# Attention and gated convolution in one launch: a new hand-out order of the same 1784 operations

## The chip, the cores and the metric

The kernel runs on one core of one Trainium2 chip. The metric is the device time of one execution in microseconds (us). The core's engines each work through a queue of their own, in order: TensorE (PE; its weight loads are shown apart as PEld), VectorE (DVE), ScalarE (ACT), GpSimd (POOL), and SyncE (SP), which issues all loads and stores. They wait for each other through semaphores, and an instruction that waits holds up everything behind it in its queue.

## What is computed

The reference is an attention with a window and a few global columns, followed by a gated convolution (B = 4, H = 8, S = 768, D = 64, local window 96, 8 global columns; model width 512, 5 taps), all in float32:

```python
scores = scale * q @ k.T + bias            # bias = -slope[h] * distance
scores = where(is_global | is_local, scores, -1e9)
a = exp(scores - max(scores)); a = a / (sum(a) + 1e-9)
x = merge_heads(a @ v)                     # [B, S, 512]
gate = sigmoid(sum_k conv_w[k] * x shifted by k)   # 5 causal taps
val = x @ w_val
out = (gate * val) @ w_out
```

Weights and tap factors arrive in 64-bit float form and are split into 32-bit numbers in the head of the kernel; the large matmuls then use a high and a low part of each factor (three matmuls for one product).

## The kernel before, in words

The rows are cut into 8 phases (4 batches, each in two halves of 3 blocks of 128 rows). A phase has 4 pairs of heads; a pair in a phase is a group (32), and a group's block is a step (96). The text names an operation by a code and its indices:

- Weights, i = 0 to 7 (0 to 3 are w_val, 4 to 7 w_out): WL loads 64-bit words; WA (L552, ACT), W1 (L557), W2 (L562), W3 (L565) and W4 (L571) on DVE make float32 of them; WH (L326 or L328) casts the high part; WS and WP make the low part, on PE (L609 to L611) and ACT or DVE for i below 4, otherwise on POOL. WL2 and SQ (L586) read them again for a check of range.
- Tables: DIST (distances; DVE, L517 and near it), BIAS(h,part) for each head (L532 on ACT, L534 on DVE or POOL).
- Attention, step s, head j of the pair: Lrk, Lrq and LV load keys, queries and values; S(u) are the scores of up to three steps (PE, L685); AM(s,j) adds the bias and takes the row minimum of the negated scores (DVE, L693); EX(s,j) is the exponential with a row sum (ACT, L704, an activation and a read of its accumulator). For two groups q and block k: RG(q,k) adds 1e-9 to the four sums (L711), RC(q,k) is the reciprocal (DVE, L714), NM(s,j) scales the row (L720), PT(q,k) transposes (PE, L734 whole, L737 in tiles), EV(q,k,i) takes it out of PSUM (L326 on ACT, L328 on the others), PV(q,k) multiplies by the values into a PSUM bank x (PE, L765).
- Convolution, group g: HI and HO carry the 4 last columns from one phase to the next (L863; L326 or L328), XH and XL are the high and the low part of x (L326 or L328, L872), CV(g,k) are the five taps (L883 the first on ACT, L881 the others on DVE), SG is the sigmoid in the form of a tanh (ACT, L928).
- Output, phase ph: VM(ph,m,c) is x @ w_val (PE, L935), GM(ph,m) the gate times it (DVE, L944), GH and GL its two parts (L326 or L328; L952), OM the second matmul (PE, L963), OE its evacuation (L975, L977), ST the store (SP, L989).

What sets the order is a list written out in full, the string `ORDER` (lines 53 to 128). `Plan.order()` walks it and emits one operation a word, so each engine's queue holds its operations in the order in which the list names them:

```python
for word in ORDER:
    i = int(word.rstrip("agvst"))
    e = self.ENGINES.get(word[-1]) or next(iter(ops[i][1]))
```

A word is the number of the operation and, where it may run on several engines, the letter of one (a ACT, v DVE, g POOL). While it walks, a cost model in `Plan.order()` guesses when each operation begins. It decides two further things: whether a transpose PT is done whole or in tiles (`self.tiled`), and where PE gets filler matmuls that multiply constants in a wait expected before 95 us: `self.fills` ahead of an operation that opens a PSUM bank, `self.before` ahead of others. No other list of priorities is consulted.

Of the kernel before, what the change touches and what calls it, by code (L numbers as in the profile page):

```python
# [61 lines left out]
    235 468 446g 1132 477 18 469g 1142 444g 449a 28 460 184g 1133 314 31 463 1126v 1137 478 470 1143 487 1152 479v  # L62
    474g 501 264 464 502 471g 196 265 451a 472g 505 452a 480 473g 506 191a 197 266 483g 488 30 205 315 1145a 489g
    509 19 484g 198 1147a 1405 36 482g 490 510 1153a 1156a 1146 192g 1399 1154a 1148 1406 496a 1157 236 200a 481g 35
    1149 495a 493g 503 494g 1158 316 20 1144a 491g 507 1155 1400 492g 195 1150 193g 1407 497a 1159 498a 1408 513 511
    1151 201g 317 504 1160 515 1401 1161v 514 1397 25 199g 1169v 523 267 524 533 534 268 516 206 512 237 517g 1402
    202g 508 1409 525 1412 518 549 526 26 550 522g 1413 499a 553 519g 554 551 1419 527v 557 521g 500a 1414 528 207
    204 532g 558 269 520v 1403g 535 531v 209a 530g 238 208v 529g 1164a 1404v 27 318 536 210g 1165 38 1172a 1420 561
    37 543a 1166 1415 552 211g 562 1421 544a 1173 1410a 1422 1416 1162a 537g 319 571 555 1411g 1423 1417a 1426 1167
    43 559 1418g 572 1432 560 42 1174 573 1427 581 1170a 538 1168 1433 556 542g 1163 545a 541g 1434 582 546a 1424g  # L70
    1175 45 1177a 539g 1428 563 1171 540g 564 239 1176 583 565g 1185v 1425g 584 566 320 597 574 598 270 567g 601
    548a 50 570v 585g 547a 568g 602 32 271 599 605 575g 44 569g 576 603 606 272 586 579g 578v 590g 580v 240 1178a
    587g 600 588g 1180v 321 1186a 577g 33 609 1429 592a 591v 1188a 49 610 1435 1179 1430a 52 619 322 620 621 1189
# [36 lines left out]
    1320 977a 1008 1633 1329 978a 1033 1011g 1034 1629 1035 1001g 1037 1324v 347 1630a 1325 1634 1015 1631 1326 1640  # L110
# [1238 lines left out]
```

## Time and profile before

| | |
|---|---|
| median of 3 runs | 251.1 us (251.1, 250.1, 251.37) |
| the profiled execution | 249.76 us, its span 248.0 us |
| instructions | 10366 |
| granted clock of TensorE, mean | 0.998 |
| PE busy | 238.8 us (96% of the span) |
| PEld busy | 204.7 us (83%) |
| DVE busy | 213.4 us (86%) |
| ACT busy | 179.6 us (72%) |
| POOL busy | 130.4 us (53%) |
| DMA | 45.94 MB, 185 GB/s on average |
| the chain that ended last | PE 80%, DVE 12%, POOL 4% of the span |

How to read it: the profile comes from one execution. Its span runs from the first to the last recorded instruction; 1.76 us of the execution's own time lie outside. An engine counts as busy while an instruction of its own is under way. L12 is line 12 of the kernel's file. The chain is followed back from the last instruction, at each step to what released it or to the instruction before it on its engine.

### The profile page before, as it was taken

Reading aid. Unit: us, or ns where it says so; the run is one execution under the profiler, and the core shown is the slowest. Engines: PE = TensorE matmul, PEld = TensorE weight load, DVE = VectorE, ACT = ScalarE, POOL = GpSimd, SP = SyncE. Lnnn points to the kernel's source line nnn. Section 1 sums busy time; section 2 is a strip of 40 time slices with the busy share of each in tenths; the row PEclk is TensorE's granted clock in tenths of the full one; section 3 lists DMA queues with packets and bytes.
Section 4 is the critical chain, followed back from the end, with each engine's and each line's share of the span. In section 5 each row is a group of like instructions: output and inputs, shape, how many; then the busy total and the mean of one; then the engine's idle time right before and its main releaser. Section 6 shows DMA issues by size and latency. Waiting matters only on the chain.

```text
span 248.0 us, 10366 instructions
## 1 busy us (share of the span) xinstructions
PE 238.8 (96%) x4037; PEld 204.7 (83%) x4041; DVE 213.4 (86%) x822; ACT 179.6 (72%) x600; POOL 130.4 (53%) x264
## 2 busy tenths in 40 slices
PE   8998788999999999999999999999999999999993
PEld 3556577888899888988899788898899889988993
DVE  3997999998979989898989989898979979989620
ACT  3999899998998488877967589886678388422202
POOL 6989999999317530364064533455419741810220
PEclk9999999999999999999999999999999999999999
DMA  5999598161298054529558289791079507200303
GB/s 181 401 397 386 200 336 284 36 187 52 61 306 306 3 186 186 167 100 272 187 172 256 84 272 345 221 312 48 7 261 402 200 25 227 73 4 0 127 8 134
DMA packets 23095, 45.94 MB, mean 185 GB/s; under 512 B 2688, under 2 KB 13696, under 8 KB 23040
## 3 DMA queue, kind: packets, MB, share of 16 engines
q1 hardware_dynamic: 23040, 45.21, 53.4%
q8 instruction: 34, 0.56, 0.9%
q14 instruction: 21, 0.17, 0.2%
HBM read 38.91 MB, written 6.29 MB: 182 GB/s over the span
## 4 chain that ended last, share of the span: by engine, by line
PE 80%; DVE 12%; POOL 4%; DMA 1%; issue 1%; ACT 0%; SPq 0%; DVEq 0%; POOLq 0%
PE o L963 26%; PE val L935 25%; PE x L765 11%; PE s L685 9%; PE pt L734 5%; PE pt L737 4%; DVE gate L881 3%; DVE t L693 3%; POOL p L720 3%; DVE wh L562 2%; DMA counts_i<-in_counts 1%; DVE xl L872 1%; DVE wy L557 1%; POOL wvh L328 1%; DVE wy L565 1%
## 5 line engine op out<-in xcount | busy, mean ns | idle before, releaser
L720 POOL TENSOR_SCALAR p<-p,rs 128x168 f32<-128x168 f32 (+1 forms) x152 | 66.3, 450 | 55.1 <-DVE rs L714 36.4
L704 ACT ACTIVATE p<-t,mins 128x168 f32<-128x168 f32 (+1 forms) x192 | 81.5, 430 | 13.8 <-DVE mins L693 12.2
L881 DVE SCALAR_TENSOR_TENSOR gate<-x,cwt,gate 128x384 f32<-128x384 f32 x128 | 76.2, 614 | 1.1
L693 DVE CUSTOM_DVE_ANT_0 t<-s,bias 128x168 f32<-128x168 f32 (+1 forms) x192 | 54.1, 318 | 7.6 <-PE s L685 7.5
L935 PE MATMUL val<-xh,wvh 128*128 128x384 f32 x128 | 44.4, 347 | 0.2 <-DVE gate L944 0.2
L326 ACT COPY a<-pt 128x384 f32<-128x384 f32 (+2 forms) x79 | 35.3, 473 | 11.7 <-PE pt L734 7.6
L935 PE MATMUL val<-xl,wvh 128*128 128x384 f32 x128 | 41.8, 327 | 0.0
L935 PE MATMUL val<-xh,wvl 128*128 128x384 f32 x128 | 41.7, 326 | 0.0
L963 PE MATMUL o<-woh,gh 128*128 128x512 f32 (+1 forms) x100 | 39.1, 391 | 0.0
L704 ACT ACTIVATION_READ_ACCUMULATOR p<-t,mins 128x1 f32 x192 | 37.6, 196 | 0.0
L963 PE MATMUL o<-woh,gl 128*128 128x512 f32 (+1 forms) x100 | 37.2, 372 | 0.0
L963 PE MATMUL o<-wol,gh 128*128 128x512 f32 (+1 forms) x100 | 37.1, 371 | 0.0
L765 PEld LDWEIGHTS x<-a,v 56*64 56x64 f32 (+1 forms) x2112 | 33.7, 135 | 4.0 <-issue 1.1
L685 PE MATMUL s<-rk,rq 64*64 64x168 f32 (+1 forms) x768 | 35.8, 304 | 1.1 <-issue 0.9
L765 PE MATMUL x<-a,v 56*64 56x64 f32 (+1 forms) x2112 | 35.8, 219 | 0.8 <-DVE x L863 0.7
L685 PEld LDWEIGHTS s<-rk,rq 64*64 64x64 f32 x768 | 25.8, 132 | 8.9 <-issue 6.0
L952 POOL TENSOR_TENSOR gl<-gate,gh 128x384 fp32r<-128x384 f32 x24 | 24.1, 1008 | 11.8 <-ACT gh L326 5.0
L935 PEld LDWEIGHTS val<-xh,wvh 128*128 128x128 f32 x128 | 24.2, 189 | 1.8 <-DVE gate L944 0.5
L935 PEld LDWEIGHTS val<-xl,wvh 128*128 128x128 f32 x128 | 24.2, 189 | 0.5 <-DVE xl L872 0.2
L935 PEld LDWEIGHTS val<-xh,wvl 128*128 128x128 f32 x128 | 24.2, 189 | 0.0
L944 DVE SCALAR_TENSOR_TENSOR gate<-gate,val 128x384 f32<-128x384 f32 x32 | 17.4, 549 | 4.7 <-PE val L935 4.5
L963 PEld LDWEIGHTS o<-wol,gh 128*128 128x128 f32 x100 | 18.9, 189 | 2.4
(101 smaller groups left out, 351.0 us busy)
## 6 DMA issues: line engine op xcount, KB each, us to landing
v<-in_vw SPq DMA_DIRECT2D x40, 384.0 KB, 5.6
rq<-in_qT SPq DMA_DIRECT2D x32, 192.0 KB, 5.3
rk<-in_kT SPq DMA_DIRECT2D x16, 252.0 KB, 4.8
out<-ob SPq DMA_DIRECT2D x15, 256.0 KB, 4.8
w<-in_wb SPq DMA_DIRECT2D x7, 512.0 KB, 5.8
again<-in_wb SPq DMA_DIRECT2D x7, 512.0 KB, 5.9
rk<-in_kT SPq DMA_DIRECT2D x16, 200.0 KB, 4.9
out<-ob SPq DMA_DIRECT2D x12, 128.0 KB, 1.8
```

The costliest lines, as they stand in the source:

```text
L326: nc.scalar.copy(dst, src)
L685: nc.tensor.matmul(T["s", step[g, k], j][half], T["rq", g][r, k * P + i * HQ : k * P + (i + 1) * HQ], T["rk", g][r, c0 : c0 + n], start=Tr ...
L693: nc.vector.tensor_tensor_reduce(out=t[:, :n], in0=T["s", s, j], in1=bias[:, h, :P] if n == P else bias[:, h, P:], op0=ALU.add, op1=ALU.mi ...
L704: nc.scalar.activation(p_of(s, j), T["t", s, j][:, :n].rearrange("p (c w) -> p c w", c=pieces(s)[0]), AF.Exp, bias=mins[:, s, j : j + 1], ...
L720: engine(e).tensor_scalar(out=pr, in0=pr, scalar1=rs, scalar2=1.0, op0=ALU.mult, op1=ALU.mult)
L734: nc.tensor.transpose(pt[n // 4][:, n % 4 * P : n % 4 * P + P], src, ident)
L765: nc.tensor.matmul(T["x", 2 * q + r][j * D : (j + 1) * D, c0 : c0 + HQ], v[rows, slot], a[rows, i, n * j + c], start=c == 0, stop=c == use ...
L881: nc.vector.scalar_tensor_tensor(out=gt, in0=src, scalar=w, in1=gt, op0=ALU.mult, op1=ALU.add)
L935: nc.tensor.matmul(T["val", ph, m], (wvh, wvh, wvl)[r][:, c, m * P : (m + 1) * P], woven((T["xh", g], T["xl", g], T["xh", g])[r][:, : size ...
L944: nc.vector.scalar_tensor_tensor(out=t, in0=t, scalar=1.0, in1=T["val", ph, m].rearrange("p (b a) -> p a b", a=2), op0=ALU.add, op1=ALU.mult)
L952: engine(e).tensor_sub(tile_of(("gl", ph, m), [P, HT], F32R, "gl", G_B)[:, :n], T["g", ph, m], T["gh", ph, m][:, :n])
L963: nc.tensor.matmul(T["o", ph, k, h], (T["gh", ph, c], T["gl", ph, c], T["gh", ph, c])[r][:, cols], woven((woh, woh, wol)[r][:, c])[:, h * ...
```

## The change

The string `ORDER` is replaced as a whole (76 lines by 76). The numbers name the same 1784 operations; nothing else in the file differs. 171 of DVE's, ACT's and POOL's operations change engine among these three (54 of them NM, 27 each way): DVE has 603 of them in place of 607, ACT 411 in place of 410, POOL 249 in place of 246; within each queue the order differs too. PE's 365 operations move by 0.33 places on average and by 7 at most, SP's 156 loads and stores by up to 18. Walking the new list, the cost model puts in 16 fillers (8 and 8) where the old list had 18 (12 and 6): two ahead of WS(2) and one each ahead of PT(1,0) and PT(1,2) are gone, two ahead of S(5) are new. One transpose in tiles is PT(13,1) where it was PT(13,2).

The first nine lines of each list and those that hold the last gate parts:

```diff
@@ -50,82 +50,82 @@
-    114 0 118 1125 1134 140 2 3 120 1g 122 123 138a 130g 119 128g 149 141 124g 142 133g 131a 143 126a 8 229 125g
-    127a 132a 7 144 135a 4 137a 357 145g 358 359 361 115 362 360 365 363 129g 116 366 158 150 146g 151 117 10 228
-    367 152 9 230 134g 364 5 153 155a 147 154g 369 370 371 379 380 372 389 381 373v 167 374 160 156 382 15 375g 390
-    148a 377v 383g 14 376g 391 161 378g 159 231 162 368 164g 384 163v 392 309 388g 157a 405 406 165 139g 407 409 176
-    387g 400a 410 136g 413 411 169 393g 16 399a 414 385g 415 170 17 232 386g 168 6 171 173g 412 394 261 172v 408 310
-    396g 166a 417 418 395g 174 185 419 427 397g 428 420 398g 437 402a 438 421g 22 429 178 422 401a 179 233 426g 430
-    11 180 175a 21 425g 311 431v 453 416 423g 432 454 262 404a 433g 457 403a 458 436g 187 439 435g 263 461 12 440
-    462 182g 188 24 455 434g 234 1129a 23 189 424g 1135a 194 441v 1138a 1130 183g 177 312 1139 1127a 465 1140 186
-    181g 13 1131 447a 29 448a 466 456 475 190g 313 1128 1136a 476 459 1398 442 485 467 443g 486 203 450a 1141 445g
...
-    1688 110 1112 1108v 1107g 1368a 1694 1113v 1095v 1366a 1685v 1689 1114 1369 1690 1116g 1367 1695 1115g 1691
-    1118g 354 1376v 1106g 111 1696 1105g 1119a 1377 1686g 1701 1120a 1378 1692a 1697 1370 1117g 1702 1374a 1693g
-    1698 355 1371 1703 1699g 1122a 1379 1708 1700g 1121v 1704 1372 1709 1375 1381a 1380 356 1389v 1710 1123a 1124v
...
+    114 0 118 140 2 3 4 120 122 123 134a 130g 138a 132g 119 149 1g 126a 142 124a 136g 141 143 127g 8 229 137a 7 144
+    125a 131g 146a 357 145g 358 359 361 115 133a 362 363 365 116 129g 366 158 150 151 128g 117 10 364 152 9 367 230
+    153 5 368 155g 228 360 147 369 154g 370 371 379 380 372 389 381 1125 167 373v 390 156 382 374 160 15 148a 377g
+    1134 135v 14 383v 375g 159 161 378g 391 231 6 162 164a 376g 384 163v 157a 387g 309 405 392 406 165 386g 407 409
+    176 388g 410 400a 17 385g 413 168 169 393g 414 411 139g 170 232 399a 11 415 171 173g 16 408 261 172v 416 310 417
+    166a 418 174 185 394 419 178 395g 427 412 428 396g 420 437 397g 401a 438 398g 421v 429 21 422 233 179 402a 22
+    423g 430 180 311 439 453 431g 426g 175a 454 262 432 182g 457 404a 187 403a 458 434g 440 461 425g 263 188 177
+    424g 24 462 194 1129a 436g 441v 189 234 23 1138a 433g 442 1130 12 183g 186 1135v 312 1131 455 1139 456 435g 465
+    1127a 181g 1140 448a 466 447a 475 203 467 1128 313 445g 1136a 476 443g 459 1398 1132 184g 468 485 13 1126a 486
...
+    1679 1373v 1688 1075v 303 1109 223 1111 304 1110 1094 1112 1104 1684 305 1097g 1106v 110 1108g 1113v 1689 1098g
+    1114 1368a 1095v 1107g 1117v 1694 1685a 1096g 1369 1376a 1690 1686g 1370 1695 1691 354 1105g 1377 1696 1692g 111
+    1119a 1378 1701 1116g 1120a 224 1371 1118g 1697 1693g 1702 1366a 1698 355 1374a 1372 1699g 1703 1367 1121a 1700g
+    1708 1379 1381v 1122v 1704 1115g 1380 1709 226 1375 356 1678 1389v 1705 1710 1123a 1124v 1706g 307 225 1707g 308
...
```

Words that are spoken of below, with the letters of the old and the new list: RG(1,0) 421g, 421v; RC(1,0) 422; RG(0,1) 383g, 383v; RG(2,2) 489g, 489v; BIAS(5,1) 135a, 135v; WH(0) 146g, 146a; WH(1) 155a, 155g; WH(2) 164g, 164a; NM(3,0) 377v, 377g; the biases 134, 124, 125 and 133 go from POOL to ACT, 131, 127 and 132 from ACT to POOL; W1(4) 178; W2(4) 179; AM(11,1) 438; EX(8,1) 416; EX(9,1) 420; EX(11,0) 439; EV(0,2,0) 403a; PV(0,2) 263; CV(0,0) 1129a; CV(0,1) 1130; HO(0) 1126v, 1126a; HO(1) 1135a, 1135v; HI(4) 1161v, 1161a; HI(5) 1169v; GM(0,0) 1402; VM(0,2,0) 1412; AM(23,1) 534; S(5) 234; S(8) 237; PV(2,0) 267; LV(0,0) 4; GH(6,0) 1685v, 1685a; GL(6,0) 1686g; GH(6,1) 1692a, 1692g; GL(6,1) 1693g; GH(6,2) 1699g; GL(6,2) 1700g; NM(92,0) 1115g; PT(15,2) 356.

## Rows read from the trace of the kernel before

**Rows 1.** Busy time of each engine in stretches: stretch, length, busy (instructions), granted clock, DMA, GB/s

```profile
7.00:20.80 13.80, 12.59 (x160) 7.84 (x155) 13.49 (x68) 13.22 (x52) 12.38 (x20) 1.00 1.04 394
...
22.60:46.50 23.90, 20.69 (x526) 16.43 (x519) 23.75 (x94) 22.61 (x77) 23.16 (x37) 1.00 0.70 250
...
46.50:228.00 181.50, 181.47 (x3224) 161.92 (x3225) 165.72 (x633) 134.85 (x454) 85.08 (x176) 1.00 0.51 169
```

**Rows 2.** Waits of DVE, 0 to 60 us: waiting line, releaser, us, times, longest

```profile
DVE rs L714 <- POOL sm L711: 1.3, 1, 1.3
```

**Rows 3.** Timeline of DVE: start, us, instruction, count, idle before and releaser

```profile
20.76 0.44 DVE L557 TENSOR_SCALAR wy<-w 128x512 int32<-128x512 int32 x1
22.55 0.18 DVE L714 RECIPROCAL rs<-sm 128x4 f32<-128x4 f32 x1 [1.35 <-POOL sm L711]
22.64 0.66 DVE L562 SCALAR_TENSOR_TENSOR wh<-w,wy 128x512 int32<-128x512 int32 x1
...
27.36 1.13 DVE L881 SCALAR_TENSOR_TENSOR gate<-x,cwt,gate 128x384 f32<-128x384 f32 x2
```

**Rows 4.** Timeline of POOL, 20 to 23 us

```profile
20.52 1.72 POOL L720 TENSOR_SCALAR p<-p,rs 128x168 f32<-128x168 f32 x4
22.32 0.20 POOL L711 TENSOR_SCALAR sm<-sm 128x4 f32<-128x4 f32 x1
```

**Rows 5.** Timeline of ACT, 20 to 26 us

```profile
20.05 0.39 ACT L704 ACTIVATE p<-t,mins 128x128 f32<-128x128 f32 x1
...
23.66 0.86 ACT L326 COPY a<-pt 128x384 f32<-128x384 f32 x2 [0.53 <-PE pt L737]
24.40 0.45 ACT L704 ACTIVATE p<-t,mins 128x168 f32<-128x168 f32 x1
...
24.83 0.43 ACT L704 ACTIVATE p<-t,mins 128x168 f32<-128x168 f32 x1
...
25.67 0.57 ACT L883 ACTIVATE gate<-x,cwt 128x384 f32<-128x384 f32 x1
```

**Rows 6.** Timeline of DVE, 44 to 46.7 us

```profile
44.81 1.19 DVE L562 SCALAR_TENSOR_TENSOR wh<-w,wy 128x512 int32<-128x512 int32 x1
45.93 1.01 DVE L944 SCALAR_TENSOR_TENSOR gate<-gate,val 128x384 f32<-128x384 f32 x2
```

**Rows 7.** Timeline of PE near 46.5 us

```profile
46.53 0.43 PE L935 MATMUL val<-xh,wvh 128*128 128x384 f32 x1 [0.16 <-DVE gate L944]
```

**Rows 8.** Waits of PE, whole span

```profile
PE pt L737 <- POOL p L720: 1.5, 3, 0.7
PE s L685 <- issue: 0.9, 1, 0.9
...
PE x L765 <- DVE x L863: 0.7, 1, 0.7
```

**Rows 9.** Groups by shape, ACT, 0 to 60 us: instructions, busy us, mean ns, idle before

```profile
L326 ACT CAST woh<-wh 128x512 fp32r<-128x512 f32 x3 | 1.9, 644 | 0.0
```

**Rows 10.** Groups by shape, DVE, 0 to 60 us

```profile
L517 DVE TENSOR_SCALAR dist<-rel,cf 128x168 f32<-128x168 f32 x1 | 0.3, 302 | 0.0
```

**Rows 11.** Line L711, 0 to 60 us: ns (min/median/max), first and last start

```profile
L711 DVE TENSOR_SCALAR sm<-sm x5: 150/237/365, 12.5 to 47.8; 128x4 f32<-128x4 f32 x5
```

**Rows 12.** Timeline of POOL, 211 to 218 us

```profile
211.97 1.94 POOL L720 TENSOR_SCALAR p<-p,rs 128x168 f32<-128x168 f32 x5 [0.63 <-DVE rs L714]
213.87 1.02 POOL L952 TENSOR_TENSOR gl<-gate,gh 128x384 fp32r<-128x384 f32 x1
...
216.19 0.51 POOL L328 CAST gh<-gate 128x384 fp32r<-128x384 f32 x1
216.77 1.01 POOL L952 TENSOR_TENSOR gl<-gate,gh 128x384 fp32r<-128x384 f32 x1
```

**Rows 13.** Timeline of PE near 218.5 us

```profile
218.49 0.82 PE L734 MATMUL pt<-ident,p 128*128 128x128 f32 x6
```

**Rows 14.** Timeline of ACT at the end

```profile
243.73 0.72 ACT L975 ACTIVATE late<-o 128x256 f32<-128x256 f32 x2 [0.41 <-PE o L963]
```

More of the change, by code (lines that the diff above doesn't have):

```diff
@@ new lines @@
+    450a 1141 28 477 235 469g 196 446g 449a 29 470 463 1133 444g 460 1142 190g 478 314 1137 487 1143 1152 464 479v
+    501 471g 264 18 451a 197 473g 265 452a 30 502 488 480 472g 198 266 191a 474g 505 489v 506 484g 490 315 1145a 509
+    481g 205 1147a 483g 1405 510 1153a 1154a 1148 482g 495a 1406 491g 1146 1156a 35 1399 494g 1149 496a 31 492g 236
+    200a 1155 192g 19 1157 1144a 503 316 195 1150 1400 493g 1158 507 201g 498a 1407 1151 497a 1408 1159 504 193g 317
+    513 508 1160 20 1161a 1401 515 514 36 1169v 1397 199g 523 267 524 533 534 268 206 516 237 525 1402 517g 202g 511
@@ new lines @@
+    1409 1412 512 518 549 38 550 526 1413 520v 519g 37 500a 527v 1419 553 521g 25 499a 554 522g 1414 535 528 557 204
+    530g 269 558 531v 529g 209a 207 1403g 238 208v 1164a 532g 1172a 318 1404v 210g 536 561 1420 562 543a 26 1165
+    544a 1415 42 1173 551 211g 1421 43 1410a 1416 1422 555 1166 319 552 537g 1423 1411g 1162a 1426 571 563 538 1174
+    1417a 539g 1432 572 573 1418g 44 581 1427 1170a 1167 27 559 1433 582 541g 545a 45 1168 542g 546a 1434 1163 556
+    540g 1175 583 1428 584 1171 239 564 1176 1177a 565g 560 320 1185v 597 32 566 598 270 570v 568g 548a 601 1424g
@@ new lines @@
+    547a 602 271 574 605 569g 606 599 1425g 272 567v 603 240 33 575g 1180a 576 50 580v 1188a 579g 321 1181 578g 1429
+    591a 577v 609 592a 610 1435 585v 1430a 619 1189 322 1436a 1178v 1438 621 1179 52 600 1439 620 1186a 1437 586 629
+    622 49 1190 590g 1440 607 588g 34 630 1445 631 593v 587g 1441 594a 589g 1187 632 1182 241 1442a 1183 611 323
+    1184 604 608 1452 623v 645 596a 646 633g 1446 39 1191 612 1453 57 1192 51 1447 1193 649 1444 1454 1202 650 613v
+    1448 614 653 616g 654 1455 40 595v 647 617g 273 1449 242 1456 1450g 56 618v 274 1457g 657 658 275 624 615v 628g
@@ new lines @@
+    1459 627g 1197a 41 626g 324 1206a 1194v 667 1451g 1460 1195v 639a 1203v 1466 648 668 1458g 1196 1461 651 677 659
+    1467 678 625g 1198 660 1462 655 46 1468 1463 1431 679 1469 1207 640a 1464g 1473 656 1470 661g 652 1465v 1474
+    1471a 634 1208 1479 680 1472g 1209 669 1475 47 670 1210 635g 59 325 662 636g 638v 1204a 1476 664v 681g 641a 637g
+    1199 642a 243 666g 1477a 1200 665g 671g 1205 326 672 1201 48 1485 673g 644a 1478 1211 693 1220 1480 58 694 695
+    697 643a 698 276 682 699 685v 277 683g 696 701 675g 702 278 674v 684g 663v 686g 244 121 1215a 676v 703 327 63
@@ new lines @@
+    705 1221a 704 706 53 1481 1213a 715 64 688a 716 1486 725 1222a 1443 1216 1224a 1482 726 700 687v 727 245 1225
+    1483a 1226 707 328 1227 708 1487 66 690a 741 709g 54 1214 689a 1492 1223 1488 742 1217 1493 1489a 1212v 710 329
+    1218 717 711g 71 745 1499 718 1219 728 1494 719v 1229a 720 1500 1228 743 724g 1495 744 1237v 746 714g 691a 1501
+    749 722g 750 747 280 713g 73 712v 692a 721g 1484 751 246 1491 281 753 754 279 763 755 764 78 729v 1496 330 1232a
+    65 723v 1502 1240a 55 773 1233 756 1506 730 775 1503 757g 1507 734g 736a 1234 1508 1497a 733g 758 774 731g 1230a
@@ new lines @@
+    1513 735a 1498g 1509 765 1514 766 1510 60 732g 331 1238a 1231 759g 760g 1504v 1515 738a 1235 1520 761g 737a 1236
+    752 1516 748 1505v 247 61 1517 767g 70 1511g 1241 332 1490 1512g 789 1521 790 791 793 739a 1518g 794 1526 1242
+    740a 1519g 792 797 1522 768 1245a 1243 776 770g 1527 798 72 762g 1239 1523 777g 1244 772g 248 1253v 1524a 795
+    284 801 796 802 778 803 283 811 77 779v 804 780v 62 282 805g 782g 806 333 771v 1248a 781g 769v 1528 813 1256v
+    784a 1532 812 783a 821 799 1257 1529 1246a 822 1533 1258 67 1530a 1249 334 823 1531 1250 1534 79 786a 1251 800
@@ new lines @@
+    1539 785a 1252 1535 68 1259 249 80 1536a 1260 1254v 335 1538 837 1546 1247 1255 1540 824 838 1547 808v 69 814
+    841 1541 787a 1525 1261 842 815g 1548 788a 825g 816 84 1270 820v 839 1542 826 845 840 1549 829g 846 843 809v
+    818g 287 1543 847 828g 810v 819g 848 250 830v 817g 1544v 807v 285 849 286 850 86 859 1553 85 860 1265a 1550 336
+    1263a 869 1274v 1262a 1551g 1554 831a 1545g 1275 1560 851 1555 844 1266 852 1552g 1561 1267 87 832a 1556 870 74
+    861 1276 853g 1562 854 337 1557 856g 1558v 1563 827g 833a 1268 1567 1559g 834a 1264 1272a 251 1269 1271a 1564 75
@@ new lines @@
+    338 1277 91 1565g 1568 1537 1279 885 836a 1566g 1273 887 1573 886 862 889 857g 871 1278 1569 872 1288 858v 1574
+    835a 76 890 873v 888 1570 863v 212 864 891 874 893 92 290 875g 894 895 877v 878g 1571v 288 855g 289 865g 868g
+    252 866g 1283v 876g 1280v 339 1292a 897 1281a 898 1575 907 1289a 880a 213 899 94 1579 867v 879a 93 908 1576
+    1290a 1284 81 909 340 917 900 1293 1577a 1580 901g 918 881a 1294 1581 896 902 1295 892 1586 903g 882a 1285 906g
+    1582 1286 82 253 1583a 214 1287 910 98 1296 341 919 911g 933 1593 920 912 1282 883a 1587 934 921g 1585 915g 922
@@ new lines @@
+    1297v 1594 1291 916g 1588 937 926g 938 924g 1595 1305v 935 941 905g 942 1589 936 914g 1596 884a 904g 1590 100
+    939 254 913g 1597 940 923g 925g 342 945 946 947 291 955 956 948 965 293 943 949g 966 105 928a 950 215 292 927a
+    83 951g 944 1591v 99 255 1300a 216 1592g 967 1301 343 968 953g 1302 1600 957 952g 930v 1298a 969g 1601 954g 981
+    1299 1607 1598g 983 982 1602 929a 1599g 985 101 1306a 1303 1608 1603 344 1604 1609 986 1605a 1304 1614 1308a 989
+    1606g 106 932a 990 1610 218 931v 987 1615 1611 1572 345 1309 88 1612a 1620 1578 1310 988 1613g 107 984 1616 1311
@@ new lines @@
+    976a 1621 1312 958 1313a 1307 1617 959g 960 217 1321a 256 963g 975a 89 961g 296 220 964g 993 1618v 995 962g 294
+    994 1619 1003 996 295 970 1584 973v 1005 974g 997v 1004 346 972g 1316a 1013 998 1622 1014 1324a 1317 1000g 978a
+    999g 1626 219 971g 1314v 1623 222 1318 108 1322a 1627 977a 1624v 90 257 1006 1319 991 1315 1628 992 1002v 1015
+    1323 1633 1007v 1325 1629 1320 347 1630a 1326 1634 1029 1631 1001v 1640 1031 1030 1625 1008 1327 1641 1032 95
+    1009g 1635 980a 1329 1328 1642 1338 1033 1632 1636 1034 1037 1643 1038 298 1035 1637 1016 96 258 979v 1036 1017g
@@ new lines @@
+    1638v 297 1018 1041 299 1022g 1644 1019g 1042 1647 1051 1639g 1333a 348 1645a 1334 1648 97 1646g 1024a 1335 1654
+    1342a 1052 1649 1331a 1061 1020g 221 1023a 1655 1010g 1053 1062 1650 1039 1012v 1011g 1656 1021v 1040 1651 259
+    1339a 102 1336 1652g 113 1332 349 1653g 112 1340v 1657 1026a 1025v 1661 1341 1077 350 1658 1079 1662 1343 103
+    1028a 1659g 1330a 1344 1043 1667 1660g 1063 1078 1663 1345 1027a 1044 1668 1346 1054 1337 1664 1064 1055g 1347
+    1045v 1356 1669 1065v 1081 1665a 1046 1056 300 1082 1083 1047g 1666 1085 302 1049g 1086 1066 1048g 1059v 301
@@ L129 @@
+    1752 1768 1753v 1756 1747v 1761 1754g 1757 1783 1762 1769 1763 1758 1764 1759 1774 1765 1760 1770 1775 1771 1766
+    1776 1777 1772 1778
 """.split()
```

70 lines of the change are left out of this document (6 added, 64 removed).

## The prediction

> **What bounds the kernel now.** I read the busy time by stretches first [rows 1]. From 46.5 to 228 us TensorE (PE) is busy 181.47 of 181.50 us: nothing done on another engine can shorten that stretch, it can only open a hole in it. From 228 us on, the last matmuls and stores follow. So the time is made of three parts: how late PE gets into its unbroken run, the run itself, and the tail. The reader is to see in [rows 1] that before 46.5 us it is the others that are full: from 7 to 20.8 us DVE 13.49, ACT 13.22 of 13.80 us, and from 22.6 to 46.5 us DVE 23.75 of 23.90, while PE leaves 23.90 - 20.69 = 3.21 us unused. I take the head as one long DVE queue with one large hole.
>
> The hole heads the list of DVE's long waits for another engine [rows 2], and stands among its instructions [rows 3]. W1(4) ends at 20.76 + 0.44 = 21.20 us; then DVE stands still for 1.35 us until RC(1,0) at 22.55 is released by RG(1,0) on POOL. POOL's queue shows why [rows 4]: RG(1,0), 0.20 us long, stands behind four NM that run from 20.52 for 1.72 us. What it needs is older: EX(9,1) starts on ACT at 20.05 and is done near 20.5 [rows 5].
>
> At the end of the head, GM(0,0) runs on DVE at 45.93 right behind W2(7) [rows 6], and PE's VM(0,2,0) at 46.53 waits for it, by 0.16 us only [rows 7]. PE's waits before that are POOL's NM (1.5 us in 3 pieces), an x bank on DVE (0.7) and 0.9 us in which the profile shows nothing that it waited for [rows 8]; no load is among them. These are also on the DVE and POOL queues, so PE can follow if those get earlier.
>
> **The change part by part.** Both lists name the same 1784 operations. PE keeps its 365 in almost the same order (on average a place moves by a third of a position), so its work is unchanged but for fillers: 18 become 16. Two ahead of WS(2) and one each ahead of PT(1,0) and PT(1,2) go, two more stand ahead of S(5). They lie in PE's waits; I cost them at nothing. If S(5) were ready earlier, the two would delay it, but 0.9 us of unexplained wait falls on its last matmul anyway.
>
> *The hole.* RG(1,0) moves to DVE, right behind AM(11,1), so POOL is out of this path. If EX(9,1) is there in time, the whole 1.35 us go.
>
> *What DVE gets for it.* Ahead of RG(1,0): BIAS(5,1) and RG(0,1) come, NM(3,0) goes. A bias on DVE has no row; the nearest is the distance row of the same shape and kind, 0.30 us [rows 10]; below, nothing, as it can't be free; above, twice that if POOL holds it up. I take 0.30. RG on DVE took 0.15 to 0.37 us [rows 11]; I take 0.15, the undisturbed one. NM(3,0) is a bias-like instruction, 0.3. Net +0.15: DVE is free for RG(1,0) at 21.35.
>
> *What ACT gets.* Ahead of EX(9,1): WH(0) and WH(2) in place of WH(1), four biases in place of four others, and EX(8,1) moved in front. A weight cast on ACT takes 0.64 us [rows 9], an exponential with its accumulator read 0.43 (from 24.40 to 24.83 [rows 5]); together +1.07. ACT had 13.80 - 13.22 = 0.58 us unused up to 20.8, part of which WH(0) can fill as it now stands ahead of the first exponential. So EX(9,1) ends between 21.0 and 21.6; I take 21.4. RG(1,0) then runs at 21.55 and RC(1,0) at 21.70 instead of 22.55: **-0.85 us**, of the 1.35.
>
> *What is late next.* EV(0,2,0) has WH and EX(11,0) in front of it, again +1.07, against 0.53 us that ACT stood idle for PT(0,2) at 23.66 [rows 5], and the 0.58 from before. PT(0,2) itself should come earlier, as POOL's NM(2,x) and NM(5,x) have less in front. So EV(0,2,0) lies between 0 and 0.55 us later; I take 0.4. PV(0,2) and then CV(0,0), at 25.67 before, follow: 26.07, done at 26.64. DVE comes to CV(0,1), at 27.36 before [rows 3] and with RC(1,2) now in front, some 0.75 us earlier, that is about 26.6: it loses 0.1. From there to GM(0,0), HO(1) and RG(2,2) come to DVE and HO(0) and HI(4) go: even. W2(7), 1.19 us against 0.66 for W2(4) [rows 3, 6], is a slow one; nothing says it will be quicker. So GM(0,0) is some 0.65 us earlier. PE reaches VM(0,2,0) through PV(2,0), PV(2,1) and S(8), which hang on HI(4) (now on ACT), HI(5) and AM(23,1); ACT is the engine with more to do. I take **-0.5 us** for PE's entry into its run; bounds: +0.5 (ACT as late as 1.07, and its waits passed on to DVE) and -1.5 (the whole hole, and the POOL wait of PE with it).
>
> *Loads.* In SP's queue the values LV(0,0), LV(0,2), LV(1,0) move ahead of weights and keys. The first is 128 KB, 0.3 us at the 394 GB/s of that stretch [rows 1], and what stands behind it has no wait for a load in before [rows 8]. Stores move by up to 18 places too; Lrk(18) now stands behind Lrq(21), which waits for S(17). Cover: in PE's list 14 other operations stand between S(17) and S(18). I cost it at nothing; if the cover doesn't reach, PE waits for the whole rest of the load.
>
> *The run.* PE's holes there are 0.03 us, so the gain is zero. The largest risk is NM(92,0): POOL did it before GL(6,0), now it stands behind GL(6,2), and PT(15,2) at 218.49 needs it [rows 13]. Before, POOL went from GL(6,0) at 213.87 to the end of GL(6,2) at 217.78, that is 3.91 us [rows 12]. The new list has in that stretch GH(6,1) (0.5, as GH(6,2) took) and, counting NM(92,0), three NM more at 1.94 / 5 = 0.39: 5.6 us. Starting at 213.87 it would end at 219.5 and cost PE 1.0 us. But those five NM, from 211.97 on, stood in front of GL(6,0), and none of them does now: GL(6,0) can start up to 1.9 us earlier, as soon as ACT has done GH(6,0) (DVE's before). I put that near 212.3, and the end of NM(92,0) near 217.9. Bounds 0 and +1.0; I take 0.
>
> *Tail.* The last two evacuations start with the last matmul, 243.73 [rows 14], in both lists. 0.
>
> Sum: the profiled execution took 249.76 us for a span of 248.0; 249.76 - 0.5 = 249.26. The median of the runs shown is 251.1, 1.34 above that execution, so I forecast **250.6 us**.
>
> **Rivals.**
>
> *The whole hole goes* and PE's POOL waits with it: 1.35 us, plus what ACT does not take. For it: PE leaves 3.21 us in the head. Against: ACT's added 1.07. About 1.4 less: 249.7.
>
> *ACT takes the hole over.* If no idle time absorbs the 1.07 us, CV(0,0) ends at 27.3, DVE waits there for 0.7 of the 0.85 won, and SG(0) and HI(4) are late as well. The order then changes nothing: 251.0.
>
> *The moved instructions wait for POOL* (slower). Five small ones come to DVE in the head (BIAS(5,1), RG(0,1), RG(1,0), RG(2,2), HO(1)) while POOL is at 23 of 24 us. If each stands behind one whole NM, 1.72 / 4 = 0.43 [rows 4], that is 2.15 us: 250.6 + 2.15 = 252.7. It decides from 0.5 us in all, where the gain is gone. For it: RG on DVE took up to 0.37, W2(7) 1.19. Against: the median RG on DVE is 0.24, an excess of 0.09 and not of 0.43. The Trainium skill, "SBUF — State Buffer", section "Who interferes with whom", speaks for this rival: a DVE instruction in a two-port mode, or with two SBUF inputs, and a GpSimd one exclude each other, and the loser waits for the whole instruction. By that rule the sum would be this rival's; the rows so far show a fraction of it.
>
> *POOL's queue at 214 to 219* (slower, small): the 1.0 us above against 0.5 won: 251.6.
>
> **How the numbers follow.** 0.5% is 1.25 us, about what a measurement of this kernel can tell from no change: 249.85 and 252.35 are the borders. Chances: my forecast 0.45 (its own spread 249.8 to 251.4), the whole hole 0.20, ACT 0.17, the wait for POOL 0.10, the queue at 214 us 0.08. Faster: two thirds of the second (0.14) and a quarter of the first (0.12): 0.26. Slower: all of the fourth but a little (0.08), a third of the last two cases that end between (0.05), and holes of the run that I have not seen (0.06): 0.19. No change: 0.55. The range must reach the whole hole below and the wait for POOL above without taking in all of either: 249.3 to 252.5.
>
> **What would show it.** Right: RC(1,0) starts near 21.7 with under 0.4 us of wait before it; VM(0,2,0) starts near 46.0; PE from there to 228 us is without holes. Wrong: a new DVE wait for ACT at CV(0,1) or XL(0) of over 0.5 us; RG on DVE over 0.4; a PE wait for POOL before PT(15,2), or one for a load before S(18) or PV(14,2). A hole in PE's run that I did not look for is what would make the forecast wrong by most.

## The result, and the profile after

The new list is slower: 253.99 us median of 6 runs (252.35 to 254.49) against 250.17 us (249.55 to 251.37); ratio 1.0138, 95% interval [1.0112, 1.0165]. The forecast was 250.6 us, with 249.3 to 252.5 as range. The profiled execution took 254.34 us, its span is 252.3 us, 4.3 more than before.

Busy time by stretches after the change, same columns as [rows 1]:

```profile
7.00:20.80 13.80, 12.20 (x162) 7.75 (x164) 13.37 (x64) 13.17 (x50) 12.07 (x19) 1.00 1.04 396
22.60:46.50 23.90, 20.45 (x520) 16.47 (x515) 23.46 (x95) 22.89 (x81) 22.51 (x37) 1.00 0.66 236
46.50:228.00 181.50, 180.38 (x3216) 160.29 (x3215) 161.89 (x619) 132.95 (x451) 88.04 (x183) 1.00 0.52 171
```

The third row is the surprise: PE has 1.12 us of holes in a run that had 0.03. The four longest of its waits over the whole span, the answer to [rows 8]:

```profile
PE pt L737 <- POOL p L720: 1.5, 2, 1.0
PE val L935 <- DVE flag L1091: 1.3, 1, 1.3
PE pt L737 <- ACT a L326: 1.1, 1, 1.1
PE s L685 <- issue: 0.8, 1, 0.8
```

The second is new and stands near the end: a matmul waits for `flag`, the value that decides whether the branch at the kernel's end is taken. The fourth has no releaser, as in [rows 8], but now it is late in the run. Where PE starts the same operation in both traces (PE has the same operations ahead of each of these) shows where the 4.3 us came in:

| PE starts | before | after | difference | added since the row above |
|---|---|---|---|---|
| VM(0,2,0), the run's begin | 46.53 | 45.99 | -0.54 | -0.54 |
| the first PV(13) | 197.55 | 197.37 | -0.18 | +0.36 |
| PT(14,0), right behind S(31) | 200.46 | 201.45 | +0.99 | +1.17 |
| PT(15,1) | 215.57 | 217.01 | +1.44 | +0.45 |
| VM(7,3,1) | 234.54 | 237.50 | +2.96 | +1.52 |
| the last matmul | 243.75 | 246.79 | +3.04 | +0.08 |
| end of the span | 248.0 | 252.3 | +4.3 | +1.3 |

The head did what was forecast. DVE's timeline, the answer to [rows 3]: RG(1,0), RC(1,0) and W2(4) follow each other, without the 1.35 us of standing.

```profile
21.57 0.17 DVE L711 TENSOR_SCALAR sm<-sm 128x4 f32<-128x4 f32 x1
21.77 0.18 DVE L714 RECIPROCAL rs<-sm 128x4 f32<-128x4 f32 x1
21.86 0.73 DVE L562 SCALAR_TENSOR_TENSOR wh<-w,wy 128x512 int32<-128x512 int32 x1
```

PE's timeline holds the three losses of the run, each by the bracket behind its row, at S(31), at PT(15,1) and at VM(7,3,1); the brackets are 2.45 us of the 3.14 us that the table has for these three.

```profile
199.17 0.45 PE L685 MATMUL s<-rk,rq 64*64 64x168 f32 x2
200.44 1.08 PE L685 MATMUL s<-rk,rq 64*64 64x168 f32 x22 [0.82 <-issue]
...
217.01 0.84 PE L734 MATMUL pt<-ident,p 128*128 128x128 f32 x6 [0.29 <-ACT xh L326]
...
237.50 0.40 PE L935 MATMUL val<-xh,wvh 128*128 128x384 f32 x1 [1.34 <-DVE flag L1091]
```

**The flag.** Four operations that the forecast never costed make it: FA (a maximum over all row minima, DVE), FB (a transpose, PE), FC (seven small instructions on DVE, L1085 to L1091) and FV, which reads the flag into a register of every engine. FV's place in the list is therefore a wait in PE's queue too. The old list has FC ahead of GM(7,0), done at 230.73, and PE reads the register at 232.01. The new list puts FA just ahead of GM(7,0), FC behind GM(7,1) and FV ahead of VM(7,3,1); the flag is done at 236.91, and all five engines read it between 236.94 and 236.95, since all five were waiting. FC on DVE, with what POOL does meanwhile (timeline of both):

```profile
234.76 0.27 DVE L1085 TENSOR_REDUCE far<-rmt 1x1 f32<-1x128 f32 x1
...
234.97 0.50 POOL L328 CAST gh<-gate 128x384 fp32r<-128x384 f32 x1 [12.94 <-DVE gate L944]
...
235.12 0.36 DVE L1087 SCALAR_TENSOR_TENSOR slow<-counts,slow 1x1 f32<-1x1 f32 x1
...
235.56 0.99 POOL L952 TENSOR_TENSOR gl<-gate,gh 128x384 fp32r<-128x384 f32 x1
...
235.70 0.86 DVE L1089 SCALAR_TENSOR_TENSOR slow<-far,slow 1x1 f32<-1x1 f32 x1
...
236.77 0.14 DVE L1091 CAST flag<-slow 1x1 int32<-1x1 f32 x1
```

An operation on a single number takes 0.86 us at L1089, and ends at 236.56, when POOL's 0.99 us at L952 end (236.55); L1087 ends with POOL's cast in the same way (235.48 and 235.47).

### The profile page after: what moved, and what is told of

Same layout as the page of the kernel before. It is cut to its first block, busy times and chain, and to the rows that moved or that the text cites. A ratio compares the mean times of both kernels' runs of the same rounds, so it can differ in the third digit from the quotient of the medians.

```text
span 252.3 us, 10363 instructions
## 1 busy us (share of the span) xinstructions
PE 238.4 (94%) x4036; PEld 204.2 (81%) x4039; DVE 213.0 (84%) x818; ACT 179.2 (71%) x601; POOL 131.1 (52%) x267
## 4 chain that ended last, share of the span: by engine, by line
PE 77%; DVE 9%; ACT 6%; POOL 3%; issue 2%; DMA 1%; SPq 0%; DVEq 0%
PE o L963 23%; PE val L935 22%; PE x L765 13%; PE s L685 10%; PE pt L734 5%; PE pt L737 4%; DVE gate L881 3%; ACT p L704 3%; POOL p L720 1%; DMA counts_i<-in_counts 1%; DVE t L693 1%; ACT gate L928 1%; DVE gate L944 1%; DVE wh L562 1%; ACT wvl L326 1%
## 5 line engine op out<-in xcount | busy, mean ns | idle before, releaser
L720 POOL TENSOR_SCALAR p<-p,rs 128x168 f32<-128x168 f32 (+1 forms) x152 | 65.5, 446 | 29.7 <-DVE rs L714 24.2
L693 DVE CUSTOM_DVE_ANT_0 t<-s,bias 128x168 f32<-128x168 f32 (+1 forms) x192 | 55.2, 320 | 8.0 <-PE s L685 7.6
L326 ACT COPY a<-pt 128x384 f32<-128x384 f32 (+2 forms) x82 | 36.7, 474 | 11.5 <-PE pt L737 5.6
L704 ACT ACTIVATION_READ_ACCUMULATOR p<-t,mins 128x1 f32 x192 | 38.6, 201 | 0.0
L765 PE MATMUL x<-a,v 56*64 56x64 f32 (+1 forms) x2112 | 36.6, 220 | 1.4 <-DVE x L863 0.5
L952 POOL TENSOR_TENSOR gl<-gate,gh 128x384 fp32r<-128x384 f32 x27 | 27.1, 1007 | 10.4 <-DVE gh L328 4.8
L711 POOL TENSOR_SCALAR sm<-sm 128x4 f32<-128x4 f32 x28 | 5.8, 209 | 45.1 <-ACT p L704 43.1
L883 ACT ACTIVATE gate<-x,cwt 128x384 f32<-128x384 f32 x29 | 16.2, 587 | 15.9 <-PE x L765 15.8
```

The source lines that it names most:

```text
L326: nc.scalar.copy(dst, src)
L693: nc.vector.tensor_tensor_reduce(out=t[:, :n], in0=T["s", s, j], in1=bias[:, h, :P] if n == P else bias[:, h, P:], op0=ALU.add, op1=ALU.mi ...
L704: nc.scalar.activation(p_of(s, j), T["t", s, j][:, :n].rearrange("p (c w) -> p c w", c=pieces(s)[0]), AF.Exp, bias=mins[:, s, j : j + 1], ...
L720: engine(e).tensor_scalar(out=pr, in0=pr, scalar1=rs, scalar2=1.0, op0=ALU.mult, op1=ALU.mult)
L765: nc.tensor.matmul(T["x", 2 * q + r][j * D : (j + 1) * D, c0 : c0 + HQ], v[rows, slot], a[rows, i, n * j + c], start=c == 0, stop=c == use ...
L883: nc.scalar.mul(gt, src, w)
```

## The experiments

Twelve kernels ran. Most undo one part; the numbers in their lists are the words of `ORDER`. Medians are given with the ratio to the kernel before on the same chip.

**The flag early.** New list, three words moved.

```diff
-    1388 1734 1779 1726 1729
...
-    1736 1731 1780 1737 1732v
...
-    1742 1738 1781 1743 1739g
...
+    306 227 1779 1714 1384a
...
+    1386 1727 1780 1387 1724a
...
+    1730 1736 1781 1731 1737
```

> The new list, with FA, FB and FC (the flag that the branch at the end reads) put back to where the old list has them: FA right behind SQ(7), FB behind VM(7,0,0), FC ahead of GM(7,0). Theory A (PE's 1.34 us before VM(7,3,1) is the wait for the flag): the hole goes, 254.0 - 1.3 to 1.6 = 252.4 to 252.7; if the last store then also lands sooner, down to 251.3. Rival B (something else was due there anyway, GL(7,0) or GM(7,2)): PE stands as long at OM(7,2,1,0), 253.6 to 254.1. The stand of 0.82 us in S(31) stays under both.

251.82 us, 1.0066 [1.0037, 1.0095]. PE's stand for the flag is gone and nothing takes its place; theory A holds and B falls. The gain, 2.2 us by the medians and 1.8 by the two ratios, is larger than the stand: PT(15,1) does not wait in this trace, and the tail (from the end of the last matmul to the end of the span) is 4.7 us long instead of 5.2. The stand in S(31) is there again, 0.82 us at the same place.

**The flag late, in the old list.**

```diff
-    1124v 307 1779 1705 308
...
-    1727 1724a 1780 1388 1728 1734 1781 1726 1729
...
-    1733g 1742 1782 1739v 1743 1713 1748 1725 1744 1719 1749
...
+    1728 1734 1779 1726 1729
...
+    1736 1731 1780 1737 1732g
...
+    1741 1738 1781 1733g 1742
...
+    1739v 1743 1748 1744 1782 1713 1725 1719 1749
```

> The old list, with FA, FB, FC, FV and the three stores of phase 6 as late as in the new one; nothing else of it changes, so GH(7,1) and GL(7,1) stay on DVE. Theory A: FC ends about 1.2 us after GM(7,1) at 232.86, that is 234.1, and PE reads the flag 0.6 us later, 0.2 to 0.5 us after VM(7,3,1) was due at 234.54: 250.4 to 250.7; were FC as long as in the new list (2.15 us), 251.5. Rival B: 250.2, no change.

250.57 us, 1.003 [1.0007, 1.0052], in theory A's range. The trace shows less: PE stands 0.1 us before VM(7,3,1) at 234.86, and enters its run at 46.71 instead of 46.53, which the edit does not touch. So in the old list the late flag by itself costs little, and the 1.34 us of the new list need more than lateness. POOL is at work here too: of FC's instructions L1087 takes 0.37 us, and ends at 233.56 with POOL's L952 (233.55).

```profile
232.55 1.00 POOL L952 TENSOR_TENSOR gl<-gate,gh 128x384 fp32r<-128x384 f32 x1
...
233.19 0.37 DVE L1087 SCALAR_TENSOR_TENSOR slow<-counts,slow 1x1 f32<-1x1 f32 x1
```

**POOL kept away from the flag.** New list, flag late, two words moved (GH(7,1) 1739, GL(7,1) 1740).

```diff
-    1742 1738 1781 1743 1739g 1748 1740g 1744 1782 1749 1745 1773 1725
+    1742 1738 1739a 1781 1743 1748 1744 1782 1749 1745 1740v 1773 1725
```

> The new list with the flag as late as it has it, but POOL kept free while DVE works it out: GH(7,1) goes to ACT and GL(7,1) to DVE behind GM(7,2). Theory P (two of FC's seven small instructions, 0.86 and 0.36 us, waited for POOL's GL(7,1) and GH(7,1)): each of FC's instructions takes under 0.3 us, FC 1.2 instead of 2.15 us, PE's stand before VM(7,3,1) 0.3 to 0.5 instead of 1.34, 254.0 - 0.9 = 253.1. Rival (they were slow for another reason, such as a fetch of DVE's instructions): the same two stay long, 254.0.

253.17 us, 1.0127 [1.0112, 1.0141]. The times cannot carry theory P, since the changed kernel's 1.0138 lies inside this interval; the trace does. DVE's and PE's timelines of this kernel: the same two instructions take 0.15 us, and PE waits 0.41 instead of 1.34.

```profile
234.91 0.15 DVE L1087 SCALAR_TENSOR_TENSOR slow<-counts,slow 1x1 f32<-1x1 f32 x1
...
235.27 0.15 DVE L1089 SCALAR_TENSOR_TENSOR slow<-far,slow 1x1 f32<-1x1 f32 x1
```

```profile
236.35 0.40 PE L935 MATMUL val<-xh,wvh 128*128 128x384 f32 x1 [0.41 <-issue]
```

**New list with the old tail.** From VM(7,0,0) on, what is left stands in the old order.

```diff
-    (new list, words 1721 to 1784)
+    (the same operations in the old list's order and with its letters)
```

> The new list up to VM(7,0,0), then what is left in the old order: flag early, GL(7,1) on DVE, the old order of the last matmuls. Theory A with the order of the last matmuls as cause of the longer tail: 254.0 - 1.4 - 1.3 = 251.3. If the tail's 1.3 us come from something that is not in the list: 252.6. Rival B: over 253.

251.76 us, 1.0046 [1.0023, 1.007]: between the expectations. The tail is 4.0 us, but the cut put FA so late that FB waits 0.63 us for it (`PE rmt L1079 <- DVE row_max L1074`), which the edit had not meant to change. The stand of 0.82 us in S(31) is there.

**The last matmuls in the old order**, on the kernel with the flag early.

```diff
-    1773 1725 1750 1746a 1719 1767 1751 1713 1755 1752 1768 1753v 1756 1747v
-    1761 1754g 1757 1783 1762 1769 1763 1758 1764 1759 1774 1765 1760 1770 1775
+    1767 1725 1750 1746a 1719 1755 1751 1713 1756 1747v 1752 1773 1753v 1757
+    1761 1754g 1768 1783 1762 1758 1763 1774 1764 1759 1775 1765 1760 1769 1770
```

> The kernel with the flag early, and PE's operations of phase 7's VM and OM in the old list's order, with GL(7,2) ahead of GM(7,3) as there. The tail from the last matmul's end to the span's end was 3.7 to 4.0 us in the traces with the old order and 4.7 and 5.2 with the new. Theory O (the order of the last matmuls decides how the last stores meet an instruction fetch): tail 3.7 to 4.1, 251.8 - 0.7 = 251.1. Rival (the tail is longer for what happens before): tail 4.7 to 5.2, 251.8.

251.2 us, 1.0051 [1.0036, 1.0066]; the tail is 3.9 us. The ratio does not stand clear of 1.0066, the kernel's without this edit, but the traces do: over all of them the tail is 3.7 to 4.2 us with the old order of these matmuls (ten traces) and 4.7 to 5.4 us with the new (the changed kernel, the two with the flag early and no other order, and the one with POOL kept away), so theory O holds for the cause in the list. What lies between is argued from packets. SP's waits at the end of the changed kernel:

```profile
SPq L1345 <- DMA out<-late: 3.2, 3, 2.2
```

It waits 2.2 us for the last store alone. Nearly all packets of that store have moved by 249.4 us; a 16 KB instruction fetch is under way from 248.78 to 250.24, and the last 8 packets move only behind it, by 250.94. In the kernel before, the corresponding fetch starts at 246.48, when the last store is nearly through. That the packets stood behind the fetch was not tried by itself.

**A shift of PE's instruction stream.** Three kernels put 16, 4 and 8 small matmuls behind the warm-up, the first on the kernel with the flag early, the others on the one with the old order of the last matmuls as well; a fourth puts 16 into the old list. In the new list they run while PE waits for the first loads: with 16 of them the first scores begin at 7.03 us, without at 6.99. In the old list PE has no such wait, and the first scores move from 6.70 to 7.30. In the cut, `ones_...` stands for a constant tensor of ones.

```diff
-    plan.add(("WARM",), -100, {PE: 3.44 + 0.22 * (WARM - 8)}, lambda e: zeros(WARM))
+    def shift(n):
+        for _ in range(n):
+            nc.tensor.matmul(T["warm",][:, :16], ones_128x128, ones_128x16, start=True, stop=True)
+    plan.add(("WARM",), -100, {PE: 3.44 + 0.22 * (WARM - 8)}, lambda e: (zeros(WARM), shift(16)))
```

> The kernel with the flag early (new list, FA, FB and FC as in the old one), and behind the warm-up matmuls 16 more of 16 columns each, so that all of PE's later instructions stand 32 places further on in its stream; the warm-up waits for data there anyway. Theory F (PE stands 0.82 us in the middle of S(31) because the fetch of its next instructions comes late, and the fetch comes when PE's queue crosses a fixed place of the stream): 32 instructions earlier the crossing lies ahead of the wait at the first PV(13), the stand goes, S(31) ends 1.0 to 1.2 us sooner, 251.8 - 1.1 = 250.7; another such stand can turn up elsewhere. Rival D (a wait for data that the profile doesn't name): the stand stays where it is, 251.8.

> The kernel with the flag early and the old order of the last matmuls (251.2), with 4 matmuls of 16 columns more behind the warm-up: 8 instructions of shift. Theory F: a fetch of PE's instructions comes when its queue crosses a fixed place of the stream; it now crosses it right behind the wait at the first PV(13), and a few instructions earlier it would lie ahead of that wait. If 8 are enough the 0.8 to 1.1 us in S(31) go: 250.1 to 250.3. If not, 251.2, unchanged. Rival D' (the stand belongs to the extra work at the head, not to the place in the stream): nothing changes with 8, and nothing with 16.

> The same with 8 matmuls more, 16 instructions of shift. Theory F: the stand in S(31) goes; 32 instructions brought a new one of 1.47 us at a transpose near 212.7, here it is smaller or absent: 250.1 to 250.7. Rival D': 251.2.

> The old list itself with 16 matmuls of 16 columns more behind the warm-up, 32 instructions of shift, and nothing else changed. Theory F: that the old list has no such stand in its run is a matter of where its instructions lie, and another place can cost it up to 1.5 us: 250.2 to 251.6, with every PE stand of over 0.3 us that the profile gives no releaser for 1 to 2 us behind the start of a fetch. If the old order cannot be hurt in this way: 250.0 to 250.3 and no new stand.

With 16: 252.72 us, 1.0132 [1.0102, 1.0162]; with 4: 250.43 us, 1.0029 [1.0016, 1.0043]; with 8: 250.77 us, 1.0045 [1.0028, 1.0062]; the old list with 16: 250.34 us, 1.003 [1.0007, 1.0053]. In none of the three shifted new lists does S(31) wait. PE's waits, for 16, 4 and 8 in this order (added lines moved the numbers by 5):

```profile
PE pt L739 <- issue: 1.5, 1, 1.5
```

```profile
PE val L940 <- issue: 0.7, 1, 0.7
```

```profile
PE val L940 <- issue: 0.8, 1, 0.8
```

Eight instructions take away a stand of 1.07 us that is 190 us later, and a smaller one turns up at 215; 32 bring one of 1.47 us at a transpose, and with them the forecast of 250.7 was missed by 2.0 us. The two smaller shifts came out 0.1 us above their ranges. That the stand moves with the place of the instructions speaks for theory F and excludes D and D'. The queue of instruction fetches, q8, shows more; that it is PE's is inferred, as PE has some 8,100 of the 10,363 recorded instructions and each other engine under 900. In the changed kernel no packet of any kind moves from 196 to 197.9 us; then comes the fetch (windows 196 to 197.9 and 197.9 to 198.2 us of the DMA view):

```profile
DMA packets 0, 0.00 MB, mean 0 GB/s; under 512 B 0, under 2 KB 0, under 8 KB 0
```

```profile
q8 instruction: 1, 0.02, 20.4%
```

With 4 matmuls more the same fetch is there at 193.4 to 193.7 us, 4.5 us earlier, long before PV(13):

```profile
q8 instruction: 1, 0.02, 20.1%
```

PV(13) and S(31) are 240 and 48 instructions in some 3 us of PE's work; PE runs dry in them if the fetch comes at 198. Over all traces: in the five with the stand in S(31) this fetch begins 0.7 to 1.0 us behind the start of PV(13), in the other nine 1.9 us or more ahead of it. All these stands end 2.2 to 2.8 us behind the start of a fetch (198.07 and 200.44; 211.97 and 214.17; 213.38 and 215.61; in the shifted old list 211.26 and 214.06, a stand of 0.42). So does the wait without a releaser in [rows 8], which the trace of before has in its head, at S(5): a fetch starts at 25.43, and the wait of 0.89 us ends at 27.97.

Place alone does not decide, though. All eight traces with the rest of the new list have in PE's run a stand of 0.73 us or more without a releaser, shifted or not; of the six with the old rest only the shifted one has such a stand, and its time is longer for a second reason, as PE enters its run at 46.95, 0.42 us late. And the new head with the old rest, below, has the same 3370 weight loads of PE ahead of PV(13) as the changed kernel, but its fetch comes at 194.23, 2.6 us ahead of PV(13), and there is no stand. So the order has a part in when the fetch comes; how, no run shows.

**The new head alone.**

```diff
-    (old list)
+    (new list, words 1 to 395, up to S(9); then what is left in the old order)
```

> The first 395 words of the new list (up to S(9), about 50 us), then what is left in the old order. If the head alone does what the prediction said, PE enters its run 0.5 us earlier and nothing is lost later: 249.5 to 249.9. Rival: the gain is lost again in the run, as 0.35 us of it are between 47 and 185 us in the new list: 250.1 to 250.4.

249.21 us, 0.9958 [0.9941, 0.9976]: faster than both lists, by more than was expected. PE starts VM(0,2,0) at 45.83, and its run has no hole (busy time of this kernel by stretch):

```profile
46.00:228.00 182.00, 182.00 (x3229) 162.39 (x3229) 166.28 (x634) 134.99 (x454) 84.59 (x176) 1.00 0.51 169
```

**RG(1,0) by itself**, moved in the old list, and moved back in the new head; the fillers are held in both.

```diff
-    402a 438 421g 22 429
...
+    429 178 421v 422 401a
```

> The old list with one word moved: RG(1,0) on DVE, right ahead of RC(1,0); the fillers are held as they were. If the 1.35 us that DVE stood there is what set PE's entry into its run, and nothing else is late: RC(1,0) at 21.35 instead of 22.55, 250.2 - 0.5 to 1.2 = 249.0 to 249.7. Rival (other engines carry the head as well, the new list's gain comes from all of its moves): VM(0,2,0) within 0.2 us of 46.53, 250.0 to 250.4.

```diff
-    438 398g 421v 429 21
+    438 398g 421g 429 21
```

> The new head with the old rest (249.2), with RG(1,0) back on POOL behind the same four NM; the fillers are held. It is done there near 22.3 (the NM end at 22.06) instead of 21.73, RC(1,0) at 22.4 instead of 21.8. Theory H (the head is one DVE queue, and the hole ahead of RC(1,0) is the part of the head's gain that matters): PE enters its run 0.5 us later, 249.7. Rival M (the gain comes from the other moves of the head, since RG(1,0) alone brought the old list 0.2 us): PE's entry moves by 0.2 us or less, 249.1 to 249.4.

In the old list 249.79 us, 1.0004 [0.9987, 1.0021]: RC(1,0) starts at 21.50, over 1 us earlier, and VM(0,2,0) at 46.31, only 0.22 earlier; DVE now stands for S(4) instead. In the new head, with RG(1,0) back on POOL, 250.0 us, 0.9996 [0.9984, 1.0008]; VM(0,2,0) at 46.37. DVE's timelines of the two (added lines moved the numbers by 2):

```profile
23.33 0.33 DVE L695 CUSTOM_DVE_ANT_0 t<-s,bias 128x168 f32<-128x168 f32 x1 [0.45 <-PE s L687]
```

```profile
22.50 0.18 DVE L716 RECIPROCAL rs<-sm 128x4 f32<-128x4 f32 x1 [0.73 <-POOL sm L713]
```

By the times, the move alone and the others alone change nothing that can be measured (1.0004 and 0.9996), and both together bring 0.4% (0.9958). PE's entry says the same: 46.31 and 46.37 against 46.53 before and 45.83 with both. Differences of 0.2 us in it are no more than traces of one head differ by: in the six traces with the new head and no added matmuls VM(0,2,0) starts between 45.77 and 46.27, in the two with the old head at 46.53 and 46.71. Both theories were half right: without RG(1,0) on DVE the gain is lost (theory H), and RG(1,0) alone does not bring it (rival M).

## Why the prediction was wrong, by its own steps

**The sum's base.** 251.1 us was the median of three runs; over six it is 250.17. As a change, -0.5 us was forecast and +3.8 measured; the high base hid 0.9 us of the miss.

**The hole and what is late next: right in the head's hole and in PE's entry, partly by luck.** RC(1,0) was put at 21.70 and stands at 21.77; EX(9,1) was to be done at 21.4 and is at 21.46; VM(0,2,0) was put near 46.0 and stands at 45.99. Farther down two errors cancel. DVE's timeline, the answer to [rows 6]:

```profile
44.50 0.82 DVE L562 SCALAR_TENSOR_TENSOR wh<-w,wy 128x512 int32<-128x512 int32 x1
45.25 1.01 DVE L944 SCALAR_TENSOR_TENSOR gate<-gate,val 128x384 f32<-128x384 f32 x2
```

GM(0,0) is 0.68 us earlier, as forecast (0.65), but W2(7) starts only 0.31 earlier and then takes 0.82 instead of 1.19, which was not expected; and VM(0,2,0) no longer waits for GM(0,0). The premise, one DVE queue with one large hole, was too simple: the hole closed alone brings nothing that the times can tell, nor do the other moves alone.

**Loads at nothing: nearly right.** PE waits for a load at 6.99 us (0.34) and perhaps at 9.96 (0.32), where the releaser named is `remote`. Both lie in the head, and PE's entry has them in it.

**The run, "so the gain is zero" with bounds 0 and +1.0: this failed.** The three places with their sizes are S(31) (+1.17), PT(15,1) (+0.45) and VM(7,3,1) (+1.52). The largest was in reach of the argument: it checked what waits for POOL and for loads, and passed over the four operations of the flag as part of "the same 1784 operations". Their words lie in the lists, 5 to 34 places later among all words than before (FA 34, FB 9, FC 12, FV 5), and FV's wait stands in each queue. Counting, in every queue, what a moved step is moved past would have found it. For S(31) the trace of before held a sign: the 0.9 us without a releaser in [rows 8], which the prediction names twice and sets aside. By its timing it is a stand of the same kind, 2.5 us behind the start of a fetch, and said that such stands can come; that one would come at S(31) it could not say.

**The rival "POOL's queue at 214 to 219": wrong as priced.** NM(92,0) is late as described and ends at 218.87, but PT(15,2) starts at 219.96, late by the losses before it, and does not wait. PT(15,1) waits 0.29 us in this trace and 0.28 in that of the old order of the last matmuls, and not at all in the one with the flag early, which has the same order there. The releaser in the bracket, ACT's cast, is not the cause: in the kernel with the flag early PT(15,1) starts at 216.44, before the second of these casts is done at 216.86 (ACT's timeline there):

```profile
216.00 0.86 ACT L326 CAST xh<-x 128x384 fp32r<-128x384 f32 x2 [0.66 <-DVE gate L881]
```

In the two that wait a fetch starts at 214.57 and 214.58, 2.4 and 2.3 us before the wait ends, in the third at 213.93. That the wait belongs to the fetch is argued, not shown.

**The rival "the moved instructions wait for POOL": the mechanism came, at another place.** In the head RG on DVE takes 0.17 us in the median (0.24 before, [rows 11]). At the flag the wait is whole: 0.86 us of L1089 in place of 0.15, and the two waits are 0.93 of the 1.34 us (1.34 - 0.41 with POOL kept away). The Trainium skill, "SBUF — State Buffer", section "Who interferes with whom", says that a DVE instruction with two SBUF inputs contends with a GpSimd instruction that reads SBUF, and that the port pair they share is an exclusive lock. The trace agrees: L1089 ends within 0.01 us of POOL's instruction. Its small size did not help, as it worked on one number.

**The tail, 0: this failed**, by 1.3 us. That the last evacuations follow the last matmul is true of both lists. What follows them is not equal, and hangs on the order of phase 7's last matmuls.

**Fillers at nothing**: nothing shows a cost in PE time. But two fillers fewer are four instructions fewer in PE's stream, and a shift of eight took PE's stands in the run from 1.35 to 0.73 us (ratio 1.0051 to 1.0029, with intervals that overlap). Whether these four matter is not shown.

**Open**: 0.36 us that PE loses between 47 and 197 us, in no hole above 0.05 us. The new head with the old rest doesn't lose them, so they belong to the rest of the new list. With this rest shifted by 8 or 32 instructions 0.1 us or less is lost there, shifted by 16 it is 0.2, so the place in the stream may have a part in it.

## What to carry to other kernels

A wait to which the profile gives no releaser is worth a look at the queue of instruction fetches before it is set aside. When a schedule is replaced, look first at the operations that occur once and are waited for by every engine (a flag, a branch, a register read): here 5 to 34 places cost 1.3 us, in a forecast that had counted them as nothing. A gain in a head was kept when only the head was exchanged; the best version here is the new head with the old rest, 0.4% faster than before. And a kernel whose PE has no slack can lose or gain up to about a microsecond by the place of its instructions in the stream, so a list that a search found is good together with its exact instruction count.

## What the runs showed of the hardware that was not expected

- The fetch of PE's instructions is not always hidden: stands of 0.4 to 1.5 us in one piece ended 2.2 to 2.8 us behind the start of one, the one in S(31) within a burst of 288 instructions. The Trainium skill, "Runtime: NRT & Kernel Launch", section "Instruction fetch mechanics", has blocks of 16 KiB refilled while the engine runs, mostly hidden. The packets agree in size (16,384 bytes, 34 in a run); that they are hidden holds in these runs for all but one to three.
- A DVE instruction on a single number took 0.86 us while POOL worked on 128x384, and 0.15 with POOL kept away.
- The one packet of such a fetch takes 0.9 to 1.8 us. A store whose last packets came meanwhile landed 1 us later; that the fetch held them up is argued from the packets.
